# One core, chunked attention, routed attention and a feed-forward layer: the attention tick as a list of single-engine operations, one order for each kind of tick

## Chip, core and metric

One core of a Trainium2 chip runs the whole program. The time is the device time of one execution in microseconds (us); lower is better. PE is the matmul engine, PEld its weight loads, DVE the vector engine, ACT the activation engine, POOL the general-purpose engine (GpSimd), SP the engine whose queue issues the DMAs.

## What is computed

The reference, cut to what matters (B = 8, H = 8, S = 576, D = 64, so 4608 rows of width 512):

```python
# 1. attention inside chunks of 64 rows, for each head
scores = scale * np.matmul(q_c, k_c.transpose(0, 1, 2, 4, 3))
attn = softmax(scores)                    # max subtracted, sum + 1e-9
x = np.matmul(attn, v_c)                  # rows of 512 = 8 heads x 64
# 2. four experts of causal attention over all 576 rows, top 2 of 4 per row
for e in range(4):
    q, k, v = x @ wq[e], x @ wk[e], x @ wv[e]
    a = softmax(where(causal, -1e9, scale * q @ k.T))
    out += gate_weight[e] * (a @ v @ wo[e])
# 3. layer norm, 512 -> 2048 -> 512 with relu, residual
return x + np.maximum(xn @ w_ch1, 0.0) @ w_ch2
```

`w_ch1` and `w_ch2` arrive as float64 and are narrowed to float32 on the core with integer operations.

## The kernel before

The 4608 rows are 36 tiles of 128 rows, nine to a pair of sequences. After a prologue the first two parts run together in **ticks**. Tick `s` (from 7 on) works on several tiles at once, each at another stage:

- chunk attention of tile `s`: scores on PE (`chunk_scores`), maximum and shift on DVE and exponential on ACT (`chunk_soft`), row sums on DVE and the scaling of `pc` on POOL (L168, `chunk_norm`), transposes on PE (`pT_ps`, L174) copied by ACT to `pTc` (L176, `chunk_turn`); then, one tick later, the values (`chunk_values`, L186, which reads `pTc`) and their split into a high part (ACT, L195) and a low part (DVE, L196);
- a share of the projections of three tiles (`proj_group`): matmuls into `pp` (L237) or `pv` (L258), then the high part on ACT and the low part on DVE (`kWl` L251, `ql` L241, for `pv` the copy `lg` L261);
- expert attention of tile `g = s - 7`: scores `sp` on PE (L345) for two pairs of experts, mask and negated maximum on DVE (L358), exponentials on ACT (L364), sums and gate weights `l` on DVE (L373 to L375), and the weighting of `P` on POOL (L379, `attn_weigh`);
- tile `g - 1`: transposes of `P` into `tp` on PE (L390), copied out half by ACT (L392) and half by DVE (`pTa`, L394);
- tile `g - 2`: values `oa_ps` on PE (L409), their high part `zh` on ACT and low part `zl` on DVE (L412), then the output projection `y_ps` (L419), copied by ACT (L422) and sent off by SP.

The number of key blocks differs: a tile has one to five of 128 keys, by its place in its pair of sequences. Ticks in which the scores are over 512 columns wide (the fifth and the ninth tile of each pair of sequences) are **wide**: their second pair of experts is scored late in the tick, after the transposes, since each wide score tile takes a buffer of its own. Every third tick has a third projection step.

PSUM, the matmuls' output memory, is shared in two pools: `pss` has three buffers (`sp`, `sx_ps` of the chunk attention, `tp`), `ps` has two (`pT_ps`, `pp`, `pv`, `oa_ps`, `y_ps`). A matmul into a buffer waits until the readers of its last contents are done.

In ticks 7 to 36 the order on PE, DVE, ACT and POOL is the order in which `tick` is written (`manual_schedule`); an instruction that waits holds up all that stand behind it on its engine. SP's DMAs are placed by a scheduler. Ticks 37 to 44, in which the layer norm of the third part is begun (`fill`), and the third part itself are ordered by the scheduler on all engines.

The narrowing of `w_ch1`, 16 blocks of 128x512, runs in the ticks' background (`narrow`, called through `bg`, seven steps a tick): a load, four DVE steps (L438, L440, L442, L444), an addition on POOL (L446), two DVE steps (L451, which waits for the addition, and L456), two multiplications on ACT (L460), four combinations on POOL (L469), a store. One block is begun when the one before it is finished, 16 steps later; what is left at the end of tick 36 is put out there at once (`bg(s, 999)`). The narrowing of `w_ch2` runs in the third part and uses the same helper.

The heart of the order before is:

```python
        if last:
            zhigh, zlow = attn_values(g - 2)
            zhigh()
        ...
        if live:
            attn_weigh(g, 0, 1 if late2 else EP)
        if zlow:
            zlow()
        if s < NT:
            chunk_norm(s)
```

Of the kernel before, what the change touches and what calls it, by code (L numbers as in the profile page):

```python
# [7 lines left out]
F32 = mybir.dt.float32  # L8
# [14 lines left out]
def tile_kernel(ctx, tc, dims, qkt, vt, wqt, wkt, wvt, wo, g_ln, w_ch1, w_ch2, out):  # L23
# [118 lines left out]
    probs, turned, valued = {}, {}, set()  # L142
# [10 lines left out]
    def chunk_soft(g, acc):  # L153
        nm = se.tile([128, 2, HP], F32, name="nmc", bufs=3)
        nc.vector.tensor_reduce(nm, acc, AX.X, OP.max, negate=True)
        pc = se.tile([128, HP, 2, C], F32, name="pc", bufs=2)
        nc.vector.tensor_tensor(pc.rearrange("p h b j -> p b h j"), acc, nm[:, :, :, None].to_broadcast([128, 2, HP, C]), OP.add)
        pw = pc.rearrange("p h b j -> p (h b j)")
        nc.scalar.activation(pw, pw, AF.Exp, scale=scale)
        probs[g] = pc  # L160

    def chunk_norm(g):
        pe = probs[g].rearrange("p h b j -> p (h b) j")
        l = se.tile([128, H], F32, name="lc", bufs=3)
        nc.vector.tensor_reduce(l, pe, AX.X, OP.add)
        nc.vector.tensor_scalar(l, l, 1e-9, None, OP.add)
        nc.vector.reciprocal(l, l)
        nc.gpsimd.tensor_tensor(pe, pe, l[:, :, None].to_broadcast([128, H, C]), OP.mult)  # L168

    def chunk_turn(g):  # L170
# [4 lines left out]
        pT = se.tile([128, HP, 128], F32, name="pTc", bufs=2)  # L175
        nc.scalar.activation(pT, pT_ps, AF.Copy)  # L176
        turned[g] = pT

    def chunk_values(g, acc):
        pT, vb = turned.pop(g), loaded.pop(g)[1]  # L180
        valued.add(g)
# [6 lines left out]
    def chunk_high(g, acc):  # L188
# [6 lines left out]
        nc.scalar.activation(xh, src, AF.Copy)  # L195
        return lambda: nc.vector.tensor_tensor(xl, src, f32(xh), OP.subtract)  # L196
# [4 lines left out]
    def early_scores(g):  # L201
        acc = pair_tile(pss, "s_ps", "ps2")[:, :, :HP, :]
        chunk_scores(g, acc)
        chunk_soft(g, acc)
        chunk_norm(g)

    def early_values(g):
        acc = pair_tile(pss, "x_ps", "ps2")[:, :, :HP, :]
        chunk_values(g, acc)
        valued.remove(g)  # L210
        chunk_high(g, acc)()
# [3 lines left out]
    HALF = (slice(0, HD), slice(HD, 2 * HD))  # L215

    def proj_group(gi):
# [13 lines left out]
        def rows_(ep, isq):  # L231
            wh, wl = (wqh, wql) if isq else (wkh, wkl)
            ws = slice(ep * 128, (ep + 1) * 128)
            pp = ps.tile([128, GW], F32, name="pp", tag="ps")
# [4 lines left out]
            if isq:  # L239
                nc.scalar.activation(qh[:, ep, :], pp, AF.Copy)  # L240
                nc.vector.tensor_tensor(ql[:, ep, :], pp, f32(qh[:, ep, :]), OP.subtract)  # L241
                return
            for w, base, end in ((0, 0, WK), (1, S, 2 * S)):
                lo_, hi_ = max(t0, base), min(t0 + GW, end)
                if lo_ >= hi_:
                    continue
                kh, kl = kWs[p, w]
                src = pp[:, lo_ - t0:hi_ - t0]
                ds = slice(lo_ - base, hi_ - base)
                nc.scalar.activation(kh[:, ep, ds], src, AF.Copy)  # L250
                nc.vector.tensor_tensor(kl[:, ep, ds], src, f32(kh[:, ep, ds]), OP.subtract)  # L251

        def vals(j):
            pv = ps.tile([128, VW], F32, name="pv", tag="ps")
# [5 lines left out]
            nc.scalar.activation(vg[:, j, :], pv[:, :NV], AF.Copy)  # L260
            nc.vector.tensor_copy(lg[:, j, :], pv[:, NV:])  # L261

        for fn, arg in ((rows_, (0, False)), (rows_, (0, True)), (rows_, (1, False)), (vals, (0,)), (rows_, (1, True)), (vals, (1,)),
                        (vals, (2,))):
            fn(*arg)
            if (fn, arg) != (vals, (GT - 1,)):
                yield
# [47 lines left out]
    def attn_scores(g, ep):  # L315
# [23 lines left out]
        for si in range(len(views[0][1])):  # L339
            for x, y, first, last in ((ql, kh, True, False), (qh, kl, False, False), (qh, kh, False, True)):  # L340
                for e2 in range(2):
# [24 lines left out]
        return exps  # L366

    def attn_weigh(g, e0, e1):
        p, t, w, n = split_of(g)
# [5 lines left out]
        nc.vector.tensor_tensor(l, l, wg, OP.mult)  # L375
        for ep in range(e0, e1):
# [684 lines left out]
```

## Time and profile before

| | us |
|---|---|
| median of 3 runs (lowest, highest) | 1254.93 (1252.5, 1255.03) |
| the profiled execution, own time | 1253.89 |
| its span, first to last instruction | 1251.9 |
| PE busy | 1201.5 (96%) |
| DVE busy | 899.3 (72%) |
| ACT busy | 580.0 (46%) |
| POOL busy | 258.4 (21%) |

The prologue ends about 51 us after the span's start; ticks 7 to 36 take from there to about 424 us, ticks 37 to 44 to about 500 us, and the third part the rest. A busy share is an average over these parts. Matmuls are pipelined and their ends are modelled, so PE's idle time and the waits that ended it say more than its busy time. The granted clock is the share of full speed at which the throttle let PE run.

### The profile page before, as it was taken

What the parts mean: (1) busy time and instruction counts of PE and PEld (TensorE: products, weight loads), DVE (VectorE), ACT (ScalarE), POOL (GpSimd) and SP (SyncE); (2) the same over time, 40 slices, a digit from 0 to 9 for tenths busy, and PEclk for the clock granted to TensorE, in tenths of its full rate; (3) what the DMA queues carried; (4) which work ended last, traced back from release to release, by engine and by line L of the source; (5) the groups of instructions that cost most, each with busy time, mean ns of one, the idle gap of its engine ahead of it and who ended that gap; (6) DMA issues with size and microseconds to landing.
All of it is one profiled execution on the core that took longest, in us unless ns stands there. A gap on an engine that the chain in (4) does not pass through costs nothing.

```text
span 1251.9 us, 29166 instructions
## 1 busy us (share of the span) xinstructions
PE 1201.5 (96%) x11874; PEld 1140.7 (91%) x11874; DVE 899.3 (72%) x1837; ACT 580.0 (46%) x1115; POOL 258.4 (21%) x480
## 2 busy tenths in 40 slices
PE   7999999999999889999999999999799999999998
PEld 5888887988888777999999999999799999999998
DVE  5687877787787678777657765755797778767782
ACT  3465665565556548633334433445443333324341
POOL 2244444443443534121112111210000000000000
PEclk9999999999999999999999999999999999999999
DMA  8233333333331225655554645557864445554521
GB/s 275 89 121 108 124 126 123 115 125 118 124 108 51 90 99 191 219 183 187 171 181 158 189 163 178 167 169 250 318 193 161 152 151 162 169 175 140 165 95 41
DMA packets 95845, 191.69 MB, mean 153 GB/s; under 512 B 8544, under 2 KB 42336, under 8 KB 94816
## 3 DMA queue, kind: packets, MB, share of 16 engines
q1 hardware_dynamic: 95712, 189.83, 45.8%
q8 instruction: 93, 1.52, 0.5%
q14 instruction: 40, 0.33, 0.1%
HBM read 118.50 MB, written 71.30 MB: 152 GB/s over the span
## 4 chain that ended last, share of the span: by engine, by line
PE 50%; DMA 3%; DVE 1%; issue 0%; SPq 0%; ACT 0%; DVEq 0%; ACTq 0%
PE bb L958 16%; PE bb L768 12%; PE ad L958 12%; PE ad L768 9%; PE tp L659 1%; DMA hx<-hd 1%; DMA w2u<-w2d 1%; DMA xc<-xs 0%; DMA raw<-in_w_ch 0%; SPq L776 0%; DVE hxc L918 0%; DVE hx L917 0%; DVE xr L968 0%; SPq L931 0%; DVE u L792 0%
## 5 line engine op out<-in xcount | busy, mean ns | idle before, releaser
L768 PE MATMUL bb<-x,w1u 128*128 128x256 f32 x1728 | 217.5, 281 | 3.4 <-ACT v L789 2.2
L768 PEld LDWEIGHTS bb<-x,w1u 128*128 128x128 f32 x1728 | 209.7, 188 | 4.6 <-ACT v L789 2.6
L768 PE MATMUL ad<-x,w1u 128*128 128x256 f32 x1296 | 173.7, 283 | 0.6 <-DVE v L792 0.6
L768 PEld LDWEIGHTS ad<-x,w1u 128*128 128x128 f32 x1296 | 160.6, 188 | 1.2 <-DVE v L792 0.8
L958 PE MATMUL bb<-w2u,hn 128*128 128x256 f32 x928 | 159.9, 280 | 0.8 <-DVE xr L968 0.8
L958 PEld LDWEIGHTS bb<-w2u,hn 128*128 128x128 f32 x928 | 134.0, 189 | 1.0 <-DVE xr L968 1.0
L958 PE MATMUL bb<-w2u,hx 128*128 128x256 f32 x640 | 125.5, 283 | 0.5 <-DVE hx L923 0.5
L379 POOL TENSOR_SCALAR P<-P,l 128x128 f32<-128x128 f32 (+8 forms) x144 | 87.3, 624 | 148.4 <-DVE l L375 118.0
L364 ACT ACTIVATE P<-P,nm 128x128 f32<-128x128 f32 (+8 forms) x144 | 87.1, 607 | 48.5 <-DVE nm L358 45.1
L958 PE MATMUL ad<-w2u,hn 128*128 128x256 f32 x632 | 104.4, 281 | 0.0
L958 PEld LDWEIGHTS bb<-w2u,hx 128*128 128x128 f32 x640 | 100.9, 191 | 0.7 <-DVE hx L923 0.7
L446 POOL TENSOR_TENSOR cvt<-cva,cvt 128x512 f32<-128x512 f32 x32 | 46.7, 1459 | 257.8 <-DVE cvt L444 220.0
L958 PEld LDWEIGHTS ad<-w2u,hn 128*128 128x128 f32 x632 | 89.3, 189 | 0.0
L958 PE MATMUL ad<-w2u,hx 128*128 128x256 f32 x504 | 88.9, 280 | 0.0
L469 POOL TENSOR_TENSOR cw<-cw 128x128 f32<-128x128 f32 x128 | 60.7, 494 | 66.3 <-issue 50.8
L958 PEld LDWEIGHTS ad<-w2u,hx 128*128 128x128 f32 x504 | 74.1, 189 | 0.0
L358 DVE CUSTOM_DVE_ANT_0 P<-sp,mcaus 128x128 f32<-128x128 f32 (+7 forms) x128 | 60.2, 519 | 3.5 <-PE sp L345 3.3
L409 PE MATMUL oa_ps<-pTa,vg 128*64 128x128 f32 x928 | 59.7, 279 | 0.0
L390 PE MATMUL tp<-ident,P 128*128 128x128 f32 x464 | 57.7, 273 | 1.9 <-POOL P L379 1.9
L677 DVE TENSOR_TENSOR x<-xt,x 128x512 fp32r<-128x512 f32 x63 | 45.3, 729 | 18.9 <-ACT x L676 18.9
L390 PEld LDWEIGHTS tp<-ident,P 128*128 128x128 f32 x464 | 52.5, 141 | 4.9 <-POOL P L379 3.4
L409 PEld LDWEIGHTS oa_ps<-pTa,vg 128*64 128x64 f32 x928 | 50.7, 138 | 3.9 <-issue 1.4
(244 smaller groups left out, 2609.9 us busy)
## 6 DMA issues: line engine op xcount, KB each, us to landing
qk<-in_qk SPq DMA_DIRECT2D x36, 512.0 KB, 4.2
hn<-hd SPq DMA_DIRECT2D x34, 512.0 KB, 4.2
raw<-in_w_ch SPq DMA_DIRECT2D x32, 512.0 KB, 3.7
hx<-hd SPq DMA_DIRECT2D x29, 512.0 KB, 4.6
vb<-in_v SPq DMA_DIRECT2D x36, 256.0 KB, 4.3
xs<-y SPq DMA_DIRECT2D x36, 256.0 KB, 2.2
xc<-xs SPq DMA_DIRECT2D x18, 512.0 KB, 4.5
hd<-p SPq DMA_DIRECT2D x36, 256.0 KB, 4.2
```

Of the source, the lines that this page charges most:

```text
L358: nc.vector.tensor_tensor_reduce(dst, src, mk, -1.0, -3.0 * NEG, OP.add, OP.min, nm[:, e2:e2 + 1])
L364: nc.scalar.activation(pe, pe, AF.Exp, bias=nm[:, e2:e2 + 1], scale=-1.0, accum_out=l[:, e2:e2 + 1])
L379: nc.gpsimd.tensor_scalar(pe, pe, l[:, ep - e0, e2:e2 + 1], 1.0, OP.mult, OP.mult)
L390: nc.tensor.transpose(tp[:, i, :], P[ep][e2][:, kt * 128:(kt + 1) * 128], ident)
L409: nc.tensor.matmul(o_ps[e2 * HD:(e2 + 1) * HD, ep, :], vg[:, gk % GT, e * HD:(e + 1) * HD], pT[:, e * n + kt, :], start=(kt == 0), stop=(k ...
L446: nc.gpsimd.tensor_tensor(t.bitcast(F32), a.bitcast(F32), t.bitcast(F32), OP.add)
L469: nc.gpsimd.tensor_tensor(w[:, o, :], w[:, x, :], w[:, y, :], op)
L659: nc.tensor.transpose(tp[:, f, :], xc[:, i, f * 128:(f + 1) * 128], ident)
L677: nc.vector.tensor_tensor(t[:, 1], tsum[i], f32(t[:, 0]), OP.subtract)
L768: nc.tensor.matmul(out[:, p], w[:, kt, a, WI[i], :], x[:, b_, kt, :], start=(start and p == 0 and kt == 0 and q == 0), stop=False, skip_gr ...
L958: ins = nc.tensor.matmul(to[:, t], x[:, c, ts], w2u[i][:, w, half * 4 + c, :], start=start, stop=False, skip_group_check=True)
```

## The change

`tick` is cut into operations that each work on one engine, under short names, and the order of a tick is a string of these names. There are four strings: for ordinary ticks (`""`), for ticks with a third projection step (`"3"`), for wide ticks (`"w"`) and for wide ticks with a third step (`"3w"`). The names:

- on PE: `S0`, `S1` scores of the two pairs of experts, `C` chunk scores and values, `O` values of `g - 2`, `P` and `Q` projection, `T` transposes (with their copies), `Y` output projection, `K` chunk transposes;
- on DVE: `D0`, `D1` mask and maximum, `N` chunk maximum and shift, `X` low part of the chunk values, `z` is `zl`, `R` chunk sums, `v` low part of a projection, `L`, `L1` the sums `l`;
- on ACT: `E0`, `E1` exponentials, `H` high part of the chunk values, `Z` is `zh`, `n` chunk exponential, `a` high part of a projection, `y`, `k` the copies of `y_ps` and `pT_ps`;
- on POOL: `r` scaling of `pc`, `W`, `W1` the weighting of `P`;
- `G1` to `G3` steps of the gate, `F0`, `F1` the layer norm's steps, `B` one beat of the narrowing.

`Q` takes its PSUM buffer from the pool of three. A projection onto keys that crosses two sequences now makes both high parts first and then both low parts.

The narrowing is a table of beats instead of a chain of steps: a block begins every 13 beats and its last step stands 18 beats after its load, so that two blocks overlap at their ends. POOL's addition is at beat 5 and the DVE step that reads it at beat 9 (before: 2 steps later, now 4), the last DVE step at 10 and ACT's multiplications at 13 (before: 1 step later, now 3). `cva` has two buffers for `w_ch1`. Seven beats a tick as before; one is run before tick 7, and at most 16 after tick 36.

```diff
+    BEAT = {-2: "load", 1: "v1", 2: "v2", 3: "v3", 4: "v4", 5: "add", 9: "v6", 10: "v7", 13: "gain", 14: "s0", 15: "s1", 16: "store"}
+    PERIOD = 13
...
+    beat = [-2]
+
     def bg(s, n=1):
         for _ in range(n):
-            if s < CS:
-                return
-            if not cgen:
-                if not conv:
-                    return
-                cgen.append(conv.pop(0)())
-            if next(cgen[0], 0) == 0:
-                cgen.pop()
+            beat[0] += 1
+            for k, parts in enumerate(conv):
+                name = BEAT.get(beat[0] - 1 - PERIOD * k)
+                if name:
+                    parts[name]()
+
+    PLAN = {
+        "": "S0 S1 C D0 E0 D1 H G2 N O B Z X E1 n z R r P a v B T B G3 F0 L B Y P y a W B F1 B v K k B",
+        "3": "S0 D0 S1 E0 C H G2 D1 N E1 O X Z P G3 z n R r B a v Q a v L W B F0 T Y B y P a v B G1 B B K k F1 B",
+        "w": "S0 D0 C E0 O P Z N z n H X R r F0 S1 a D1 v E1 L B L1 Y y T B P B W B B a v W1 K B F1 B k",
+        "3w": "S0 C D0 H N E0 O Z X n P R z Q a v r a v S1 L D1 T B Y B F0 W B y E1 B P a v L1 G1 K B W1 k B B F1",
+    }
...
-        if late2:
-            attn_scores(g, 1)()
-            attn_weigh(g, 1, EP)
-        if last:
-            attn_out(g - 2)
...
+        for op in PLAN[("3" if three else "") + ("w" if wd else "")].split():
+            if op in do:
+                do[op]()
         if s == MID - 1:
-            bg(s, 999)
-        if fill is not None:
-            fill(s, 1)
+            bg(s, 16)
```

Three places in the two built programs. First PE in tick 20, a wide one, from the projection of the keys on (`tp` are the transposes of `P`, `sp` the scores). Before:

```order
L237 MATMUL pp<-xTh,wkh 128x384
L390 MATMUL tp<-ident,P 128x128 x16
L345 MATMUL sp<-kWh,ql 128x320 x2
L345 MATMUL sp<-kWl,qh 128x320 x2
L345 MATMUL sp<-kWh,qh 128x320 x2
```

And now:

```order
L358 MATMUL sp<-kWh,qh 128x320 x2
L438 MATMUL y_ps<-woh,zl 128x512
L438 MATMUL y_ps<-wol,zh 128x512
L438 MATMUL y_ps<-woh,zh 128x512
...
L409 MATMUL tp<-ident,P 128x128 x16
L273 MATMUL pv<-wvh,xTl 128x260
```

The late scores, and behind them the output projection, now stand ahead of the transposes.

Second DVE in tick 19, an ordinary one, from the chunk maximum to the copy of the transposes. Before:

```order
L155 TENSOR_REDUCE nmc<-sx_ps 128x8
L157 TENSOR_TENSOR pc<-sx_ps,nmc 128x2x4x64
L295 TENSOR_REDUCE den<-ex 128x3
L296 TENSOR_SCALAR den<-den 128x3
L297 RECIPROCAL den<-den 128x3
L196 TENSOR_TENSOR xTl<-sx_ps,xTh 128x4x128
L373 TENSOR_SCALAR l<-l 128x4
L374 RECIPROCAL l<-l 128x4
L375 TENSOR_TENSOR l<-l,wg 128x4
L412 TENSOR_TENSOR zl<-oa_ps,zh 128x256
L165 TENSOR_REDUCE lc<-pc 128x8
```

And now:

```order
L155 TENSOR_REDUCE nmc<-sx_ps 128x8
L157 TENSOR_TENSOR pc<-sx_ps,nmc 128x2x4x64
L196 TENSOR_TENSOR xTl<-sx_ps,xTh 128x4x128
L431 TENSOR_TENSOR zl<-oa_ps,zh 128x256
L165 TENSOR_REDUCE lc<-pc 128x8
L166 TENSOR_SCALAR lc<-lc 128x8
L167 RECIPROCAL lc<-lc 128x8
L264 TENSOR_TENSOR kWl<-pp,kWh 128x384
L413 COPY pTa<-tp 128x512
L308 TENSOR_REDUCE den<-ex 128x3
```

The gate's three operations on `den` and the three on `l` no longer stand ahead of `zl`; they follow the copy of the transposes.

Third POOL around tick 19. Before:

```order
L299 TENSOR_TENSOR wg<-ex,den 128x12
L379 TENSOR_SCALAR P<-P,l 128x512 x4
L168 TENSOR_TENSOR pc<-pc,lc 128x512
L446 TENSOR_TENSOR cvt<-cva,cvt 128x512
L379 TENSOR_SCALAR P<-P,l 128x640 x2
```

And now (ticks 17 and 18, where the same pair of operations stands):

```order
L171 TENSOR_TENSOR pc<-pc,lc 128x512
L479 TENSOR_TENSOR cvt<-cva,cvt 128x512
L398 TENSOR_SCALAR P<-P,l 128x256 x4
L171 TENSOR_TENSOR pc<-pc,lc 128x512
L398 TENSOR_SCALAR P<-P,l 128x384 x4
```

The scaling of `pc` now comes ahead of the weighting of `P` of the same tick.

## Rows read from the trace of the kernel before

**Rows 1.** Windows: busy us of each engine, granted clock, DMA share, GB/s.

```profile
83.00:195.00 112.00, 108.05 (x1389) 96.50 (x1386) 86.04 (x247) 66.80 (x167) 47.98 (x96) 0.98 0.35 119
195.00:308.00 113.00, 107.82 (x1396) 96.22 (x1395) 85.78 (x250) 66.97 (x168) 47.88 (x96) 1.00 0.34 116
308.00:412.00 104.00, 99.74 (x1273) 89.13 (x1271) 78.12 (x227) 60.25 (x151) 42.83 (x88) 0.98 0.28 95
412.00:500.00 88.00, 77.87 (x639) 65.68 (x638) 65.83 (x191) 55.12 (x131) 36.99 (x74) 0.94 0.37 130
```

**Rows 2.** Waits of PE from 51 to 500: total us, times, longest.

```profile
PE sp L345 <- DVE pTa L394: 7.6, 7, 2.4
PE sx_ps L186 <- ACT pTc L176: 5.3, 5, 1.8
PE y_ps L419 <- DVE zl L412: 4.0, 4, 2.1
PE pT_ps L174 <- POOL pc L168: 4.0, 2, 2.1
PE pv L258 <- DVE lg L261: 2.0, 1, 2.0
PE tp L390 <- POOL P L379: 1.9, 3, 0.9
```

**Rows 3.** Windows just behind two waits of PE, columns as in rows 1.

```profile
155.00:160.00 5.00, 4.22 (x19) 3.42 (x20) 3.83 (x12) 2.50 (x6) 0.00 (x0) 0.66 0.33 105
...
211.00:216.00 5.00, 3.86 (x66) 3.62 (x67) 2.90 (x7) 3.90 (x10) 0.00 (x0) 1.00 0.68 251
```

**Rows 4.** Timeline of PE in tick 20: start, us, instruction, idle before and releaser.

```profile
212.14 0.69 PE L186 MATMUL sx_ps<-pTc,vb 64*64 64x64 f32 x32 [1.82 <-ACT pTc L176]
...
219.19 0.41 PE L345 MATMUL sp<-kWh,ql 64*128 64x320 f32 x1 [0.50 <-DVE pTa L394]
```

**Rows 5.** Timeline of POOL in tick 19.

```profile
206.87 1.04 POOL L168 TENSOR_TENSOR pc<-pc,lc 128x512 f32<-128x512 f32 x1
207.87 1.27 POOL L446 TENSOR_TENSOR cvt<-cva,cvt 128x512 f32<-128x512 f32 x1
```

**Rows 6.** Timeline of DVE in tick 19.

```profile
201.81 0.16 DVE L295 TENSOR_REDUCE den<-ex 128x3 f32<-128x12 f32 x1
...
202.30 0.66 DVE L196 TENSOR_TENSOR xTl<-sx_ps,xTh 128x512 fp32r<-128x512 f32 x1
202.88 0.16 DVE L373 TENSOR_SCALAR l<-l 128x4 f32<-128x4 f32 x1
...
203.44 0.42 DVE L412 TENSOR_TENSOR zl<-oa_ps,zh 128x256 fp32r<-128x256 f32 x1
...
209.17 0.43 DVE L451 TENSOR_SCALAR cva<-raw 128x512 int32<-128x512 int32 x1 [2.23 <-POOL cvt L446]
```

**Rows 7.** Timeline of ACT at the end of tick 19.

```profile
210.70 0.91 ACT L460 ACTIVATE cw<-cva,gk 128x256 f32<-128x256 f32 x2 [2.00 <-DVE cva L456]
211.51 0.57 ACT L176 ACTIVATE pTc<-pT_ps 128x512 f32<-128x512 f32 x1
```

**Rows 8.** Timeline of POOL in tick 7.

```profile
56.79 1.41 POOL L379 TENSOR_SCALAR P<-P,l 128x128 f32<-128x128 f32 x4 [0.88 <-DVE l L375]
58.16 1.04 POOL L168 TENSOR_TENSOR pc<-pc,lc 128x512 f32<-128x512 f32 x1
```

**Rows 9.** Timeline of DVE behind tick 36.

```profile
425.92 0.68 DVE L440 SCALAR_TENSOR_TENSOR cva<-raw,cva 128x512 int32<-128x512 int32 x1
...
435.17 1.06 DVE L440 SCALAR_TENSOR_TENSOR cva<-raw,cva 128x512 int32<-128x512 int32 x1
```

**Rows 10.** Timeline of POOL behind tick 36.

```profile
434.83 3.89 POOL L379 TENSOR_SCALAR P<-P,l 128x512 f32<-128x512 f32 x4
```

**Rows 11.** Groups of DVE from 51 to 457: busy us, mean ns, idle before.

```profile
L440 DVE SCALAR_TENSOR_TENSOR cva<-raw,cva 128x512 int32<-128x512 int32 x16 | 12.7, 795 | 0.3
```

**Rows 12.** Waits of DVE from 51 to 500.

```profile
DVE lg L261 <- ACT vg L260: 26.3, 20, 2.9
```

More of the change, by code (lines that the diff above doesn't have):

```diff
@@ L140, in tile_kernel @@
     groups = {}
-    probs, turned, valued = {}, {}, set()
+    probs, lcs, turned = {}, {}, {}
     ROWS = (slice(0, C), slice(C, 2 * C))
@@ L209, in early_values @@
         chunk_values(g, acc)
-        valued.remove(g)
-        chunk_high(g, acc)()
+        for f in chunk_split(g, acc):
+            f()
     qTs, kWs, vgs, wgs = {}, {}, {}, {}
@@ L447, in narrow @@
[L447 to L462 removed]
+        t_ = {}
@@ L501, in tick @@
             projs.append(proj_group((s - GT - 1) // GT))
-        live, last = 0 <= g < NT, 0 <= g - 2 < NT
-        late2 = live and wide(g)
-        xlow = zhigh = zlow = exps = None
-        if live:
-            attn_scores(g, 0)()
-            if not late2:
-                exps = attn_scores(g, 1)
-        step(gates[0] if gates else None)
-        old = s - 1 in turned
-        if old or s < NT:
+        live, wd = 0 <= g < NT, 0 <= g < NT and wide(g)
+        three = (s - GT - 1) % GT == 2
@@ new lines, in tick, with scores, proj, turn_off @@
+        do, highs, lows = {}, [], []
+        def scores(ep):
+            do[f"D{ep}"], do[f"E{ep}"] = attn_scores(g, ep)
+        def proj(big=False):
+            if projs:
+                if big:
+                    wide_bank.append(1)
+                high, low = next(projs[0])
+                highs.append(high)
+                lows.append(low)
+                if big:
+                    wide_bank.pop()
+        def turn_off():
+            if projs and three:
+                next(projs.pop(0), None)
+            step(gates[0] if gates else None)
@@ new lines, in tick @@
+        if s < NT or s - 1 in turned:
+            do["C"] = chunk
+        if 0 <= g - 2 < NT:
+            do["O"], do["Y"] = values, out_
+        if 0 <= g - 1 < NT:
+            do["T"] = lambda: attn_turn(g - 1)
+        if s < NT:
+            do["K"] = turn
+        do["P"], do["Q"], do["G1"] = proj, (lambda: proj(True)), turn_off
+        do["a"] = lambda: highs and highs.pop(0)()
+        do["v"] = lambda: lows and lows.pop(0)()
+        do["G2"], do["G3"] = (lambda: step(gates[0] if gates else None)), (lambda: step(gates.pop(0) if gates else None))
```

266 lines of the change are left out of this document (137 added, 129 removed).

## Prediction

> **What bounds the kernel now.** I read the windows by stage first. From 83 to 412 us, 26 whole ticks, PE is busy for 315.6 of 329 us, and 77.9 of 88 behind that [rows 1]. No other engine comes near: DVE, the next, has 249.9 of the 329. So the matmuls set the pace, their number is not changed, and what an order can give back is PE's idle time and the clock that it loses. The third part, over half of the span, keeps its order on PE and gives nothing.
>
> Then the waits of PE [rows 2]. The six largest between 51 and 500 us sum to 24.8 us. Each is a wait for one step of another engine, not for a busy one: late scores for a copy of the transposes, chunk values for `pTc`, the output projection for `zl`, chunk transposes for the scaling of `pc`.
>
> Third, the clock. Behind the wait that ended at 155.8 the granted clock is 0.66 over five us; behind that at 212.1 it stays 1.00 [rows 3]. 0.66 of five us is a stretch of 3.4 us at 1.2 GHz, which loses (1 - 0.66) x 5 = 1.7 us of full speed. Seven such stretches lie between 51 and 500 us, each behind one of the waits of rows 2: 7 x 1.7 = 11.9. So all that can be won is 24.8 + 11.9 = 36.7 us, 2.9%.
>
> **The change, part by part.**
>
> Wide ticks. The late scores wait because the transposes just ahead of them have taken the buffers of the pool of three, and DVE copies these out late: 7 waits, 7.6 us, one of them in rows 4. Now the late scores and the output projection stand ahead of the transposes (in `"3w"` only the scores). Their two buffers were those of the first scores, which DVE reads within 2 us, behind 5 us of other matmuls. What is late next is the transposes' second buffer, which DVE's first pass over the late scores frees: that pass is done about when eight transposes are through, so I leave 0.15 us a tick, 1.0 in all. Gain 6.6.
>
> Chunk values and the narrowing. In tick 19 POOL does the scaling of `pc` and then the narrowing's addition, which ends at 209.14 [rows 5]. DVE's next narrowing step has waited 2.23 us for it [rows 6], the multiplications on ACT wait 2.00 us for the step after that, and the copy `pTc` stands behind them until 211.51 [rows 7]; PE waits 1.82 us for it [rows 4]. This is the pattern of the 5.3 us in five waits. With four beats instead of two between addition and reader, and three instead of one ahead of ACT, each step has half a tick; ACT no longer stands still ahead of `pTc`. One place is left: in `"3w"` ACT does `E1` behind `y`, and `pTc` comes out about when the next tick wants it. I leave 0.6. Gain 4.7.
>
> `zl`. DVE did the gate's `den` (0.49 us, from the first start to the next row's) and `l` (0.56) ahead of `zl` [rows 6], and `l` can wait for exponentials besides. Both now stand behind it, which is 1.05 us earlier, but one more narrowing step (0.68, the shorter of rows 9) may stand ahead in its place. The wait of 0.64 in tick 19 becomes about 0.64 - 1.05 + 0.68 = 0.3. Four waits, 4.0 us in all, leave 1.2. Gain 2.8.
>
> First ticks. The scaling of `pc` started at 58.16, right behind 1.41 us of weighting, which now follows it [rows 8]. DVE reaches the chunk sums earlier too, by the same 1.05. POOL can then begin when the sums are there, some 1.4 us sooner than before, and of 2.1 us there stay about 0.6; in tick 8, where the weighting is longer, about 0.4. Of 4.0 us there go 3.0. The price is a later weighting, which the next tick's transposes read; they come over 5 us into that tick, so it is covered unless POOL is over 3 us behind.
>
> Behind tick 36. Three of 16 narrowings ran there in one go, with DVE steps wedged between those of the attention [rows 9]. They now run inside the ticks. The longest waits of two rows above are there and are counted there; one more, `pv` for `lg`, 2.0 us, loses its cause in part, since the second projection takes its buffer from the other pool: gain 1.0. The 1.9 us of `tp` for POOL stay.
>
> The waits sum to 6.6 + 4.7 + 2.8 + 3.0 + 1.0 = 18.1. Of the seven slow stretches five should go (the three in wide ticks, the one at `zl` behind tick 36, one of the first two): 5 x 1.7 = 8.5.
>
> Against it: three more narrowings in the ticks. Six DVE steps of at most 0.795 us, the costliest kind [rows 11], are 4.8 us a block, 14 us in all. DVE has 329 - 249.9 = 79 us free in the 26 ticks, 3.0 a tick, so most of it is covered; in the shortest ticks, of 10 us, it is not. With such ticks, and waits of the new strings that no row of before shows, I charge 4 us; the bounds are 0 and, if every tick pays half a microsecond, 13. Moving PE's groups costs nothing: the number of changes between kinds of matmuls in a tick stays. The load of the first block moves ahead of tick 7, at the same place in SP's queue.
>
> DVE and POOL get in each other's way: the same narrowing step took 0.68 us alone and 1.06 us [rows 9] while POOL weighted `P` for 3.89 us [rows 10]. The Trainium skill, page "SBUF — State Buffer", section "Who interferes with whom", says that a DVE instruction with two SBUF inputs or in a two-port mode and a GpSimd one that reads SBUF exclude each other, whichever starts second waiting. The trace agrees with a hold of 0.38 us. Were every one of a block's six steps held so, it would be 2.3 us a block; the mean of rows 11 is only 0.12 above 0.68, so spread steps are held in a third of cases, and I stay with my 4.
>
> The sum: 1253.9 (the profiled execution) - 18.1 - 8.5 + 4 = 1231.3. The median of the runs is 1.0 above the profiled one: **1232 us**.
>
> **Rivals.**
>
> 1. Only the narrowing's part comes true. The strings remove waits at one place and make them at another (the transposes' second buffer, `pv` for a late `v`, `zl` behind a narrowing beat). Then go the 4.7 of `pTc`, the 2.4 and 2.1 that are the longest of two rows [rows 2] and the 1.0, with three slow stretches behind tick 36 (5.1), less the 4: 11.3, or 1244. For it: waits of PE are a few tenths, and orders of other engines shift by as much as a narrowing step. Against it: the seven buffer waits have a cause that is gone from PE's queue.
>
> 2. The gain is given back: both effects cancel within 2.5 us, 1254. This needs new waits of over half a microsecond in every tick, which a slack of some microseconds at most of the moved steps speaks against.
>
> 3. Slower: DVE's queue becomes the bound. DVE waits at the head of its queue too, 26.3 us in 20 waits for `vg` alone, 1.3 each [rows 12]; a strict new order, with more beats inside, can add such waits. If each of the 26 ticks had one more of 1.3 that reached PE, that is 34 us against 26.6 won: 1261. It decides when waits and narrowing together use up DVE's 3.0 free us a tick. Against it: `l`, which waited for ACT, and the step that waited for POOL are moved to where their input is long there.
>
> **How the numbers follow.** The forecast, 1226 to 1238, has 0.58; rival 1, to 1249, 0.24; rival 2, 0.09; rival 3, 0.09. The lower end, 1220, is near 1253.9 - 36.7 + 1.0 = 1218, when every wait goes; the upper end, 1249, takes in rival 1 and the charge of 13. Outside stand rivals 2 and 3. A measurement of this kernel can tell 0.2%, 2.5 us, from no change: faster 0.82, same 0.09, slower 0.09.
>
> **What would show it.** Right: no wait of `sp` for a copy of the transposes; chunk values without a wait over 0.5 us for `pTc`; the waits of `zl` and `pc` down to tenths; no narrowing step of `w_ch1` behind tick 36; at most two stretches at 0.66 between 51 and 500 us; the chunk attention's last tick some 12 us earlier. Wrong: new groups among PE's waits with a sum over 10 us, above all `tp` for DVE or POOL and `pv` or `pp` for a low part; DVE busy over nine tenths of a tick with PE waiting; or slow stretches that stay although the waits are gone.

## The result and the profile after

The changed kernel takes 1215.15 us in the median (1213.76 to 1216.4) beside 1254.43 for the kernel before: a ratio of 0.9689, with an interval of 0.9672 to 0.9706. The profiled execution took 1214.83 us, its span 1213.1. The forecast was 1232 us, and the time lies under the range (1220 to 1249): the sign was right, and the gain of 39 us is more than the 36.7 that the prediction called all that can be won.

PE's waits in ticks 7 to 44 of the changed kernel (us in total, times, longest) answer to [rows 2]:

```profile
PE pT_ps L177 <- DVE l L389: 3.4, 1, 3.4
PE y_ps L438 <- DVE zl L431: 2.2, 3, 1.2
PE tp L409 <- POOL P L398: 1.3, 2, 0.9
PE sp L358 <- DVE pTa L413: 1.1, 1, 1.1
PE pT_ps L177 <- POOL pc L171: 0.9, 1, 0.9
```

`sp` waits for a copy of the transposes once (7.6 us in seven waits before), the chunk values no longer wait for `pTc` (5.3 in five), `zl` is at 2.2 (4.0 in four). The chunk transposes still wait 4.3 us (4.0): this term brought nothing.

Windows of the changed kernel (columns as in [rows 1]) behind its one long wait, and at the place of [rows 3]:

```profile
65.00:70.00 5.00, 3.64 (x29) 2.87 (x32) 4.15 (x14) 1.33 (x4) 3.42 (x5) 0.54 0.31 107
70.00:75.00 5.00, 5.00 (x85) 4.71 (x80) 3.44 (x9) 4.02 (x13) 0.00 (x0) 0.78 0.47 159
155.00:160.00 5.00, 5.00 (x55) 4.79 (x52) 4.67 (x16) 3.85 (x14) 2.08 (x5) 1.00 0.75 258
```

One slow stretch is left in the ticks, of twice the length ((1 - 0.54) x 5 + (1 - 0.78) x 5 = 3.4 us lost), where there were seven of 1.7.

Now the two halves of the attention as windows: from the chunk scores of tick 7 to those of tick 35, and from there to the first matmul of the third part. Before:

```profile
51.60:402.10 350.50, 333.49 (x4258) 298.04 (x4256) 267.61 (x782) 206.02 (x517) 147.75 (x298) 0.98 0.33 113
402.10:501.00 98.90, 88.43 (x795) 75.14 (x793) 74.31 (x215) 61.51 (x148) 40.71 (x79) 0.95 0.34 121
sum 449.40, PE 421.92 PEld 373.18 DVE 341.92 ACT 267.53 POOL 188.46; mean PE 210.96 PEld 186.59 DVE 170.96 ACT 133.76 POOL 94.23
```

After:

```profile
49.70:378.50 328.80, 323.52 (x4254) 293.69 (x4252) 278.11 (x799) 205.77 (x521) 166.06 (x309) 0.99 0.37 128
378.50:465.60 87.10, 82.53 (x812) 71.07 (x810) 67.05 (x200) 64.43 (x147) 33.48 (x68) 1.00 0.32 114
sum 415.90, PE 406.05 PEld 364.76 DVE 345.16 ACT 270.21 POOL 199.54; mean PE 203.02 PEld 182.38 DVE 172.58 ACT 135.10 POOL 99.77
```

The stretch is 449.4 - 415.9 = 33.5 us shorter. PE's idle time in it falls from 449.40 - 421.92 = 27.5 to 415.90 - 406.05 = 9.9, that is by 17.6. PE's *busy* time falls too, by 15.9 us, for the same matmuls. Of that the clock explains 7 x 1.7 - 3.4 = 8.5; 7.4 are left, for the most part waits that no row of idle time shows (the section "Waits that the idle time doesn't show"). The other 5.3 us of the 38.8 by which the spans differ lie in the prologue (1.9) and the third part (3.4).

### The profile page after: what moved, and what is told of

The parts are those of the page before. It is cut to its first block, busy times and chain, and to the rows that moved or that the text cites. A ratio compares the mean times of both kernels' runs of the same rounds, so it can differ in the third digit from the quotient of the medians.

```text
span 1213.1 us, 29176 instructions
## 1 busy us (share of the span) xinstructions
PE 1182.9 (98%) x11874; PEld 1130.0 (93%) x11874; DVE 903.9 (75%) x1837; ACT 581.7 (48%) x1117; POOL 267.8 (22%) x480
## 4 chain that ended last, share of the span: by engine, by line
PE 86%; DVE 7%; DMA 3%; ACT 1%; issue 1%; POOL 1%; SPq 0%; ACTq 0%; DVEq 0%; POOLq 0%
PE bb L1023 16%; PE bb L833 16%; PE ad L1023 12%; PE ad L833 12%; PE pp L246 7%; PE pv L273 4%; PE y_ps L438 4%; PE oa_ps L428 4%; PE tp L409 3%; PE sp L358 3%; PE tp L724 2%; PE sx_ps L151 1%; DMA w2u<-w2d 1%; PE pT_ps L177 1%; DVE P L376 1%; PE sx_ps L187 1%
## 5 line engine op out<-in xcount | busy, mean ns | idle before, releaser
L381 ACT ACTIVATE P<-P,nm 128x128 f32<-128x128 f32 (+8 forms) x144 | 87.2, 608 | 44.3 <-DVE nm L376 37.0
L398 POOL TENSOR_SCALAR P<-P,l 128x128 f32<-128x128 f32 (+8 forms) x144 | 94.8, 676 | 39.7 <-DVE l L391 24.9
L509 POOL TENSOR_TENSOR cw<-cw 128x128 f32<-128x128 f32 x128 | 64.8, 526 | 57.7 <-issue 48.4
L171 POOL TENSOR_TENSOR pc<-pc,lc 128x512 f32<-128x512 f32 x36 | 37.8, 1052 | 140.0 <-DVE lc L167 83.1
```

The source lines that it names most:

```text
L381: nc.scalar.activation(pe, pe, AF.Exp, bias=nm[:, e2:e2 + 1], scale=-1.0, accum_out=l[:, e2:e2 + 1])
L398: nc.gpsimd.tensor_scalar(pe, pe, sums_[g][:, ep, e2:e2 + 1], 1.0, OP.mult, OP.mult)
L509: nc.gpsimd.tensor_tensor(w[:, o, :], w[:, x, :], w[:, y, :], op)
```

## Experiments

Chips differ a little (the kernel before had medians of 1254.4 to 1257.2 us in the six comparisons), so kernels are compared by their ratio to the kernel before on the same chip, and "us" in the table are ratio x 1254.4. Ticks 7 to 34 and 35 to 44 are the two windows above, from the profiled executions; idle time and waits are those of PE over 0.15 us in the first. The clock is not taken out: in ticks 7 to 34 it costs 6.8 us before, 3.4 in the changed kernel, and 0 (skip7, block0_late) to 8.5 (only_narrowing, only_wide) elsewhere.

| kernel | ratio (interval) | against before | ticks 7 to 34: us, idle, waits | 35 to 44 |
|---|---|---|---|---|
| before | 1 | 0 | 350.5, 16.7, 21 | 98.9 |
| only_narrowing | 0.9988 (0.9971 to 1.0005) | -1.5 | 359.8, 22.5, 24 | 88.4 |
| only_wide | 1.0015 (1.0003 to 1.0027) | +1.9 | 354.5, 21.9, 18 | 101.9 |
| only_wide_y | 0.9970 (0.9955 to 0.9985) | -3.8 | 348.7, 17.2, 25 | 102.6 |
| high_only | 0.9948 (0.9931 to 0.9966) | -6.5 | 345.4, 12.8, 21 | 101.7 |
| wide_high | 0.9915 (0.9890 to 0.9940) | -10.7 | 342.8, 15.3, 18 | 100.7 |
| three_edits | 0.9902 (0.9878 to 0.9926) | -12.3 | 352.0, 19.2, 23 | 88.5 |
| wide_back | 0.9799 (0.9783 to 0.9815) | -25.2 | 337.7, 11.0, 9 | 89.8 |
| old_narrowing | 0.9795 (0.9781 to 0.9810) | -25.7 | 332.6, 7.4, 7 | 95.4 |
| skip7 | 0.9753 (0.9731 to 0.9776) | -31.0 | 332.4, 9.3, 11 | 91.6 |
| dist_back | 0.9739 (0.9718 to 0.9759) | -32.7 | 334.1, 9.9, 8 | 87.5 |
| l_back | 0.9734 (0.9706 to 0.9763) | -33.4 | 333.4, 8.0, 7 | 87.0 |
| skip78 | 0.9719 (0.9689 to 0.9749) | -35.2 | 332.0, 7.3, 10 | 87.1 |
| block0_late | 0.9691 (0.9668 to 0.9714) | -38.8 | 327.4, 5.2, 6 | 87.3 |
| high_back | 0.9689 (0.9667 to 0.9712) | -39.0 | 331.1, 7.0, 7 | 87.2 |
| changed kernel | 0.9689 (0.9672 to 0.9706) | -39.0 | 328.9, 5.1, 3 | 87.1 |
| after_again | 0.9689 (0.9674 to 0.9705) | -39.0 | 327.4, 5.0, 3 | 87.3 |
| y_back | 0.9678 (0.9648 to 0.9709) | -40.4 | 328.2, 5.3, 4 | 86.8 |
| block0_mid_y | 0.9682 (0.9662 to 0.9702) | -39.9 | 327.0, 4.8, 5 | 87.2 |
| block0_mid | 0.9671 (0.9656 to 0.9686) | -41.3 | 325.9, 4.5, 4 | 87.2 |

### Each half alone, and each half undone

only_narrowing puts the new table of beats into the kernel before; old_narrowing puts the old chain into the changed kernel:

```diff
-    BEAT = {-2: "load", 1: "v1", 2: "v2", 3: "v3", 4: "v4", 5: "add", 9: "v6", 10: "v7", 13: "gain", 14: "s0", 15: "s1", 16: "store"}
-    PERIOD = 13
+    BEAT = {-1: "load", 0: "v1", 1: "v2", 2: "v3", 3: "v4", 4: "add", 7: "v6", 8: "v7", 9: "gain", 10: "s0", 11: "s1", 13: "store"}
+    PERIOD = 16
...
-            bg(s, 16)
+            bg(s, 999)
```

> The kernel before with the narrowing's table of beats alone (old order of every tick). Theory A (a wait of PE costs its idle row plus some 0.3 us that no row of idle time shows): it takes away the waits for pTc (5.3 us by the rows), the two longest for zl and pTa behind tick 36 (2.1 and 2.4) and half of lg (1.0), 10.8 us in 8 waits, with 8 x 0.3 = 2.4 unseen, and three slow stretches (5.1): 1254.4 - 18.3 = 1236. Theory B (the rows are complete, and what the change gained beyond them came from the narrowing, which no longer stands in DVE's and POOL's way): 10.8 + 5.1 + the 13 us that the forecast missed: 1226.

> The changed kernel with the old chain of narrowing steps (16 steps a block, the old distances, one buffer, the rest put out behind tick 36); the new strings stay. Theory A: the strings alone give what the narrowing doesn't, 39.3 - 18.3 = 21.0: 1233. Theory B: they give the row sum of the wide ticks, zl and pc, 6.6 + 0.8 + 3.0 and two slow stretches, some 14: 1240. The rival of the prediction in which only the narrowing's part comes true: 1251 or more.

only_wide moves the late scores alone in the kernel before, wide_back moves them (and in `"w"` the output projection) back in the changed one:

```diff
+        if late2:
+            attn_scores(g, 1)()
         if 0 <= g - 1 < NT:
             attn_turn(g - 1)
...
         if late2:
-            attn_scores(g, 1)()
             attn_weigh(g, 1, EP)
```

```diff
-        "w": "S0 D0 C E0 O P Z N z n H X R r F0 S1 a D1 v E1 L B L1 Y y T B P B W B B a v W1 K B F1 B k",
-        "3w": "S0 C D0 H N E0 O Z X n P R z Q a v r a v S1 L D1 T B Y B F0 W B y E1 B P a v L1 G1 K B W1 k B B F1",
+        "w": "S0 D0 C E0 O P Z N z n H X R r F0 a v L B T B S1 D1 E1 L1 Y y P B W B B a v W1 K B F1 B k",
+        "3w": "S0 C D0 H N E0 O Z X n P R z Q a v r a v L T B S1 D1 Y B F0 W B y E1 B P a v L1 G1 K B W1 k B B F1",
```

> The kernel before with one edit: in wide ticks the scores of the second pair of experts, with their mask, maximum and exponential, stand ahead of the transposes. Theory A: 7 waits of sp, 7.6 us by the rows, and 7 x 0.3 = 2.1 unseen, less 1.0 left, and two or three slow stretches (3.4 to 5.1): 1254.4 - 13 = 1241; the span without its clock loss falls by 8.7, PE's idle time by only 6.6. Theory B: the span without its clock loss falls by as much as PE's idle time, 6.6, and the time is 1243 to 1244.

> The changed kernel with the late scores and the output projection of wide ticks behind the transposes again (in the ticks with a third step only the scores); all else as changed. Theory A: waits of sp for pTa come back, some 7 of about 1 us, with 0.3 unseen each, and two or three slow stretches: 1215.2 + 13 = 1228, and the span without its clock loss grows by some 2 us more than PE's idle time. Theory B: 7.6 + 3.4: 1226, with both growing alike.

Undone, each half costs 13 to 14 us; alone, they give 1.5 and -1.9. Theory A's figures for the halves undone hold within 3 us (1233 and 1228 expected, 1230.1 and 1231.0 measured), those for the halves alone do not: the gains do not add up, and neither theory had that.

For the narrowing the table shows where it goes: in ticks 35 to 44 it gives 10.5 us in the old order and 8.3 in the new, but in ticks 7 to 34 it costs 9.3 in the old order (1.7 of it clock) and nothing in the new (332.6 us with the old chain, 328.9 with the table of beats). For the wide ticks, the first wait of PE in only_wide:

```profile
PE tp L390 <- DVE nm L358: 9.8, 5, 3.1
```

One of them:

```profile
271.88 1.09 PE L390 MATMUL tp<-ident,P 128*128 128x128 f32 x8 [2.14 <-DVE nm L358]
```

The wait of `sp` is gone and the transposes wait instead, for the buffer of the very scores that were moved, which DVE has not yet masked. This is what the prediction priced at 0.15 us a tick.

### What makes DVE late in a wide tick

DVE in that tick of only_wide (24, with a third step), up to the mask for which PE waits, and ACT ahead of it:

```profile
266.27 0.69 DVE L155 TENSOR_REDUCE nmc<-sx_ps 128x8 f32<-128x512 f32 x1 [1.56 <-ACT xTh L195]
...
271.07 0.75 DVE L358 CUSTOM_DVE_ANT_0 P<-sp,mcaus 128x576 f32<-128x576 f32 x1
```

```profile
264.91 0.76 ACT L364 ACTIVATE P<-P,nm 128x576 f32<-128x576 f32 x1
265.57 0.18 ACT L364 ACTIVATION_READ_ACCUMULATOR P<-P,nm 128x1 f32 x1
265.67 0.57 ACT L195 ACTIVATE xTh<-sx_ps 128x512 fp32r<-128x512 f32 x1
```

The same tick of the changed kernel, which starts at 246.96 instead of 262.81:

```profile
248.82 0.69 DVE L155 TENSOR_REDUCE nmc<-sx_ps 128x8 f32<-128x512 f32 x1 [0.31 <-ACT xTh L196]
```

```profile
248.19 0.60 ACT L196 ACTIVATE xTh<-sx_ps 128x512 fp32r<-128x512 f32 x1 [0.72 <-PE sx_ps L187]
248.68 0.77 ACT L381 ACTIVATE P<-P,nm 128x576 f32<-128x576 f32 x1
```

The chunk maximum waits for `xTh`, which reads the other half of the same buffer, and `xTh` stood behind the exponentials of the first pair. In the changed kernel these follow it (`"3w"`) or the maximum comes ahead of it (`"w"`): the maximum starts 1.9 us into the tick instead of 3.5. The prediction named the place on PE and did not look at ACT. Five kernels separate the two. y_back and only_wide_y vary the output projection; high_only, wide_high and high_back vary the order on ACT:

```diff
-            attn_scores(g, 0)()
+            exps = attn_scores(g, 0)
             if not late2:
+                exps()
                 exps = attn_scores(g, 1)
```

That is high_only, an edit of the kernel before; wide_high has it and the edit of only_wide. Next y_back and high_back, on the changed kernel (in high_back also `H N` behind `E0` in `"3w"`):

```diff
-        "w": "S0 D0 C E0 O P Z N z n H X R r F0 S1 a D1 v E1 L B L1 Y y T B P B W B B a v W1 K B F1 B k",
+        "w": "S0 D0 C E0 O P Z N z n H X R r F0 S1 a D1 v E1 L B L1 T B Y y P B W B B a v W1 K B F1 B k",
...
+        "w": "S0 D0 C E0 H N O P Z z n X R r F0 S1 a D1 v E1 L B L1 Y y T B P B W B B a v W1 K B F1 B k",
```

only_wide_y is only_wide with `attn_out(g - 2)` of wide ticks right behind the late scores.

> The changed kernel with one edit, in wide ticks without a third step: the late scores stay ahead of the transposes, but the output projection goes behind them again, as it was. Theory C (it is the output projection between late scores and transposes that hides DVE's pass over the late scores, whose buffer the transposes take): tp waits for the masked scores in four ticks, some 2 us each, with 0.35 a wait unseen and one or two slow stretches: 1215.2 + 12 = 1227. Theory D (the late scores alone do it, and the waits of the kernel with only that edit came from DVE's old order): 1215 to 1218.

> The kernel before with the late scores and the output projection of all wide ticks ahead of the transposes, all else as before. Theory C: of the 9.8 us in which tp waited for the masked scores some 7 go, with some unseen time and two slow stretches: 1257.3 - 12 = 1245. Theory D: DVE's old order (the gate and the sums ahead of zl) makes the output projection wait for zl instead: no gain, 1253 or more.

> The changed kernel with one edit in wide ticks: ACT does the exponentials of the first pair (E0) ahead of the high part of the chunk values (H), and DVE's chunk maximum (N) follows behind H, as before; the places of scores, transposes and output projection stay as changed. Theory E (in wide ticks it was this order on ACT that made DVE late by some 1.5 us, since the chunk maximum waits until H has read the shared buffer, and every wait of a wide tick hangs on DVE): the masked late scores come 1.5 us later and tp or y_ps wait for DVE in the eight wide ticks, about 1 us each with 0.35 unseen and two slow stretches: 1215 + 13 = 1228. The rival (it was the place of the late scores on PE, as the prediction had it): 1215 to 1218.

> The kernel before with one edit: in wide ticks the exponentials of the first pair stand behind the high part of the chunk values on ACT instead of ahead of it. Theory E: DVE does the chunk maximum 1.5 us earlier in wide ticks, and the 7.6 us in which sp waits for pTa and the waits for zl there fall by more than half: 1254.7 - 8 = 1246. The rival: nothing, 1253 or more.

> The kernel before with both edits in wide ticks: the late scores ahead of the transposes, and the first pair's exponentials behind the high part of the chunk values. Theory E: of the 9.8 us in which tp waited for the masked scores 7 go, with the 7.6 of sp gone as there: 1257.3 - 13 = 1244. The rival: the two do no more than each alone, 1250 or more.

Theory C falls for the changed kernel: there the output projection may stand on either side (y_back). In the old order it counts in part. only_wide_y is 5.7 us faster than only_wide, half of the 12 that C expected: the transposes wait for the masked scores 1.3 us in one wait instead of 9.8 in five, as C had it, but the output projection now waits for `zl` 7.9 us in nine waits instead of 4.5 in five, as D had it. High_only takes more than half of the `sp` waits away, without a matmul moved:

```profile
PE sp L345 <- DVE pTa L394: 3.6, 5, 2.4
```

So theory E holds for the kernel before: the swap on ACT gives 6.5 us, and with it the late scores, which alone cost 1.9, give 4.2 more. In the changed kernel the order on ACT does not matter (high_back; the 1228 of theory E did not come), while the place of the scores does (wide_back). That DVE has time enough there for the old order on ACT is likely, but not shown.

What else gives DVE time? l_back puts the gate's last step and the sums back ahead of `zl` in ticks that are not wide, and three_edits adds the narrowing's table to wide_high:

```diff
-        "": "S0 S1 C D0 E0 D1 H G2 N O B Z X E1 n z R r P a v B T B G3 F0 L B Y P y a W B F1 B v K k B",
+        "": "S0 S1 C D0 E0 D1 H G2 N O B Z X E1 G3 L n z R r P a v B T B F0 B Y P y a W B F1 B v K k B",
```

(l_back has the same in `"3"`.)

> The changed kernel with the gate's last step and the sums l ahead of zl and of the chunk sums again in ticks that are not wide; all else as changed. By the prediction's terms: 2.8 for zl and up to 3.0 for pc in the first ticks come back: 1219 to 1221, with PE's waits for zl and pc longer by 4 to 6 us. The rival (with all 16 blocks inside the ticks DVE is later than before the change, and the sums wait for the exponentials at the queue's head): over 1225. A third: nothing, under 1217, if DVE is ahead of PE by the microsecond anyway.

> The kernel before with three edits and none of the new strings: late scores ahead of the transposes, first pair's exponentials behind the high part of the chunk values in wide ticks, and the narrowing's new table of beats. If DVE's slack in wide ticks is what the narrowing lacked, it now gives behind tick 36 its 10 us and loses half of the 9 us that it lost inside the ticks: 1247 - 6 = 1241. If few edits give most of the gain: 1230 or less. If the rest of the list is needed for the narrowing to be free: 1246 or more.

l_back costs 5.6 us, with `y_ps` waiting 5.8 us for `zl` in six waits instead of 2.2 in three. Three_edits came out near the 1241 that the first case expected, but not for its reason: the narrowing gives 12.3 us in ticks 35 to 44 and loses 9.3 in ticks 7 to 34, all of what it lost without the edits (342.8 to 352.0). So these two edits of the wide ticks are not what makes the narrowing free. DVE's own waits at its queue's head (us, times, longest, ticks 7 to 44) fit the view that the order of DVE as a whole makes it free, but do not show it. Before, besides [rows 12]:

```profile
DVE nmc L155 <- ACT xTh L195: 21.0, 26, 2.1
DVE ql L241 <- ACT qh L240: 11.8, 10, 2.4
DVE l L373 <- ACT P L364: 11.1, 11, 1.3
DVE cva L451 <- POOL cvt L446: 10.9, 8, 2.3
```

After:

```profile
DVE lg L276 <- ACT vg L275: 23.2, 19, 2.3
DVE nmc L155 <- ACT xTh L196: 10.9, 21, 1.5
DVE ql L264 <- ACT qh L260: 4.5, 5, 1.6
...
DVE l L389 <- ACT P L381: 1.8, 3, 1.2
```

These four go from 54.8 to 17.2 us (the last has no row left). In only_narrowing they are still 42.4 (19.8, 7.9, 10.0, 4.7). DVE's busy time in ticks 7 to 34 grew by 10.5 (278.11 - 267.61 in the windows above). These sums do not tell cause from effect. DVE's idle time in ticks 7 to 44 is their length less its busy time, 449.4 - 341.9 = 107.5 us before and 415.9 - 345.2 = 70.7 after: whatever makes the ticks 33.5 us shorter, with 3.3 us more work, takes 36.8 from it. Shown is that the two edits of the wide ticks are not enough (three_edits) and that the place of the gate's last step and the sums is worth 5.6 us (l_back). Which other entries of the list let the narrowing run for nothing was not tried one by one, and stays open.

### The beats

dist_back has the old distances inside a block, a block still every 13 beats. (From POOL's addition to the DVE step that reads it they are three steps, not the two that the description of the change and the prediction give: `add` and `v6` stand at 4 and 7 in the old chain above.)

```diff
+    BEAT = {-2: "load", 1: "v1", 2: "v2", 3: "v3", 4: "v4", 5: "add", 8: "v6", 9: "v7", 10: "gain", 11: "s0", 12: "s1", 14: "store"}
```

> The changed kernel with the old distances inside a block (the DVE step that reads POOL's addition 3 beats behind it instead of 4, ACT's multiplications 1 beat behind DVE's last step instead of 3), a block still every 13 beats and nothing more behind tick 36 than before. By the prediction's second term: the waits of chunk values for pTc come back inside the ticks, some 3 us in three or four waits, with 0.37 each unseen and one slow stretch: 1215 + 6 = 1221. The rival (packing the blocks is all the gain): 1215 to 1217.

It costs 6.3 us as expected, but by other waits: `pTc` has 0.6 us in one wait; the chunk transposes' buffer waits 2.8 us for the copy of `y_ps` on ACT, and `zl` has 3.6 instead of 2.2. The distance counts, and what a late step meets on its queue was guessed wrong.

The 3.4 us wait in tick 8 was not foreseen. In tick 7 DVE did four narrowing steps ahead of the masks of tick 8 (the last row here), and all behind them came late:

```profile
55.40 1.01 DVE L465 TENSOR_SCALAR cva<-raw 128x512 int32<-128x512 int32 x1
...
57.37 0.69 DVE L468 SCALAR_TENSOR_TENSOR cva<-raw,cva 128x512 int32<-128x512 int32 x1
58.09 0.49 DVE L471 TENSOR_SCALAR cvt<-cva 128x512 int32<-128x512 int32 x1
58.61 0.73 DVE L475 SCALAR_TENSOR_TENSOR cvt<-raw,cvt 128x512 f32<-128x512 uint32 x1
...
59.74 0.41 DVE L376 CUSTOM_DVE_ANT_0 P<-sp,mcaus 128x256 f32<-128x256 f32 x1
```

```profile
66.36 1.11 PE L177 MATMUL pT_ps<-ident,pc 128*128 128x128 f32 x4 [3.36 <-DVE l L389]
```

Three kernels take those steps away: skip7 (no beat in tick 7, all blocks seven beats later), skip78 (none in ticks 7 and 8, a block every 12 beats, and a beat moved behind `zl`), block0_late (the first block alone seven beats later, with second buffers for the raw block and `cvt`; its line of beats is shown):

```diff
-                name = BEAT.get(beat[0] - 1 - PERIOD * k)
+                name = BEAT.get(beat[0] - 1 - (PERIOD * k or 7))
```

> The changed kernel with no beat of the narrowing in tick 7, so that seven more are put out behind tick 36; beats 13 apart and all strings as changed. In the kernel without beats in ticks 7 and 8, tick 8 fell from 11.96 to 8.26 us and PE's wait in it from 3.36 to 1.08, but it lost 6 us in later ticks, where beats every 12 stood at other places. Expected: tick 8 shorter by 3 us, tick 9 by 1.1 without the slow stretch, behind tick 36 up to 1 us more: 1215.2 - 3 = 1212. The rival (any shift of the beats against the ticks makes waits, three steps of a tick in 39 being as near as they were): 1218 or more.

> The changed kernel with no beat of the narrowing in ticks 7 and 8 (a block every 12 beats instead of 13 makes up for it), and in ordinary ticks the first beat behind zl instead of ahead of it. The wait of 3.36 us in tick 8 is late by the four narrowing steps (2.9 us) that stand ahead of DVE's masks there: it falls by some 2 us, and the slow stretch behind it (up to 3.4 us long lost at half speed, 1.7) may go; the wait of 0.77 for zl in tick 19 goes. Expected 1215.2 - 2.0 - 0.8 - 0.4 = 1212, 1210 if the slow stretch goes. The rival: the first ticks are bound by the chunk attention's chain of steps from scores to transposes, and the wait stays: 1214.

> The changed kernel with the first of the 16 blocks 7 beats, one tick, later than its place in the table, and two buffers for the raw block and for cvt so that it may overlap the second; every other beat stands where it stood. Ticks 7 to 9 as in the kernel without beats in tick 7: 27.4 instead of 32.2 us, since DVE no longer does four narrowing steps ahead of the masks of tick 8; tick 9 or 10 loses up to 1.0 by the steps that now stand there; from tick 11 on as the changed kernel. Expected 1215.2 - 4 = 1211. The rival (later ticks make new waits as with the other shifts): 1218.

All three shorten tick 8 from 12.0 to 8.3 us. skip7 and skip78 lose more than that in ticks 12 to 34 (7.3 and 8.1 us). skip7 loses 4.5 more in ticks 35 to 44, 3.4 of it clock; seven more beats are put out behind tick 36 there. PE's waits in skip7 begin with these:

```profile
PE y_ps L438 <- DVE zl L431: 4.7, 5, 1.7
PE sx_ps L187 <- ACT pTc L179: 2.8, 2, 2.3
```

That beats now stand at bad places in the later ticks is read from such waits and was not tried by itself. block0_late gives 3.4 us back at once, in ticks 10 and 11: six DVE steps of two blocks now stand in tick 9, ahead of the masks of tick 10. From tick 12 to 34 it takes 273.4 us, as the changed kernel does. block0_mid spreads the steps, beside the changed kernel itself on the same chip (block0_mid_y has y_back's edit as well):

```diff
+    BEAT0 = {-2: "load", 5: "v1", 6: "v2", 7: "v3", 8: "v4", 9: "add", 12: "v6", 13: "v7", 16: "gain", 17: "s0", 18: "s1", 19: "store"}
...
+                name = (BEAT if k else BEAT0).get(beat[0] - 1 - PERIOD * k)
```

> The changed kernel with the steps of the first block of the narrowing alone spread otherwise: its four DVE steps from the last beat of tick 7 through tick 8, the addition behind them, the last two DVE steps at the end of tick 8 and the start of tick 9; two buffers for raw block and cvt; all other beats as changed. If the steps ahead of the masks were the cause: ticks 7 to 9 fall from 32.2 to about 27.5 us, ticks 10 and 11 stay within 0.5 of 23.2, and the time is 4 us under the changed kernel on this chip: 0.9660 of before. The rival (each place in these ticks costs as much as it gives): within 0.2% of the changed kernel, as block0_late.

> The same with the output projection of wide ticks without a third step behind the transposes. The kernel with that edit alone came out 1.4 us under the changed kernel, less than a measurement can tell: as block0_mid within 2 us.

> The changed kernel itself on this chip: a ratio to before of 0.9672 to 0.9706, as first measured; its prologue and its third part, where the profiled run stood 1.9 and 3.4 us under before, within the spread of the other kernels (prologue 49.7 to 53.1, third part 746.0 to 751.4), so that these 5 us belong to the run and not to the change.

block0_mid takes 1213.41 us (1213.25 to 1214.42), the changed kernel there 1215.67 (1215.53 to 1217.02): the fastest kernel, 2.3 us under it at the medians, although the intervals of the ratios overlap. Ticks 7 to 9 fall to 28.3 us from 32.2 (31.2 in after_again), but tick 10 still grows by 1.0 (1.4), with a wait of 1.19 for `zl`; 0.5 at most and a time 4 us lower had been expected. So the steps ahead of the masks were the cause in tick 8, and a quarter to a half of what they cost there comes back. block0_mid_y took 1214.27, within 2 us as expected.

### Waits that the idle time doesn't show

Tick 20 in wide_back and in the changed kernel, PE from the late scores to the output projection:

```profile
211.28 0.41 PE L358 MATMUL sp<-kWh,ql 64*128 64x320 f32 x1
212.88 0.41 PE L358 MATMUL sp<-kWh,ql 64*128 64x320 f32 x1 [1.20 <-DVE pTa L413]
...
213.95 0.50 PE L438 MATMUL y_ps<-woh,zl 128*128 128x512 f32 x1
```

```profile
204.58 0.41 PE L358 MATMUL sp<-kWh,ql 64*128 64x320 f32 x2
204.83 0.31 PE L358 MATMUL sp<-kWl,qh 64*128 64x320 f32 x2
...
205.66 0.50 PE L438 MATMUL y_ps<-woh,zl 128*128 128x512 f32 x1
```

From the first of these matmuls to the output projection it is 2.67 us with the wait and 1.08 without: the wait cost 1.59, its row says 1.20. Undisturbed, the row of the first two matmuls is shown 0.41 us long and the next row starts 0.25 after it: shown lengths overlap, and the part of a wait that falls under the last matmul shown counts as busy. Over all 20 profiled kernels of this study, the length of ticks 7 to 34 less PE's idle time and the clock's loss is 319.6 + 0.35 x (number of waits over 0.15 us), with a correlation of 0.97. By this line 18 waits fewer are worth 6.2 us that no row lists.

The kernels with many waits are those with the old order, so the line alone does not say that the waits are the cause. The traces do, step by step. Take the distance between the starts of two matmuls with a wait between them, less the wait's row, less the same distance undisturbed at full clock: it is 0.07 to 0.41 us, 0.20 in the mean of 227 waits. In ticks 7 to 34 this sums to 5.1 us for the 21 waits of the kernel before and to 0.6 for the three of the changed one. Delays too short for a row give another 1.5 us, and the undisturbed distances of the two orders of PE differ by 0.6 in sum. So the 0.35 holds more than what lies under a wait's own row, and tick 20 is near the top of the range.

## Why the prediction was wrong, by its own steps

- **Where to look** was right: the third part and the prologue are not changed. The 1.9 us of the prologue are no gain: in another run of the same kernel (after_again) it took 52.8 us, beside 49.7 here and 51.6 before. Third parts of all kernels lie between 746.0 and 751.4, in the mean 749.4 with the old order of the ticks and 747.7 with the new strings, so 1 or 2 us there may belong to the change. With the ticks (33.5 us, 34.6 in after_again) that is less than the 39 us of the medians: some 3 to 4 us are not placed.
- **The sum of the waits** came out, 18.1 forecast and 17.6 measured, but in part by luck: the terms miss by up to 3.3 us and cancel. Wide ticks: 6.6 forecast, 6.5 by the rows. `pTc`: 4.7, and 5.3 came. `zl`: 2.8, and 1.8. First ticks: 3.0, and -0.3; the narrowing's steps ahead of the masks of tick 8 were left out of this term. `pv`: 1.0, and 2.0. These make 15.3; 0.6 came at `tp` for POOL, which was to stay, and 1.7 at waits outside the six rows.
- **The clock** was right in sum: 5 x 1.7 = 8.5, and 8.5 came. By stretches it was not: six went and the one that is left is twice as long (in after_again it is 1.7).
- **The ceiling failed.** 24.8 + 11.9 was called all that can be won, since idle time was taken for the whole price of a wait. Beyond idle time and clock PE's busy time fell by 7.4 us more, most of it the parts of waits that no row shows.
- **The charge of 4 us failed.** It was reckoned from DVE's free time of 3.0 us a tick as if that were slack, to be paid for the most part in the shortest ticks. In the old order the three blocks cost 9.3 us in ticks 7 to 34 (only_narrowing), in the new one nothing could be seen of them. What in the new list does this stays open beyond the 5.6 us of l_back.
- 17.6 - 18.1 = -0.5 for the waits, 4.0 for the charge, 7.4 for what no row shows and 5.3 outside the ticks make the 16.2 us by which the profiled span lies under the sum. The first three are steps of the prediction, 10.9 us together; the 5.3 are none.
- **The cause in wide ticks** was half right: buffers and place on PE as named, but alone they move the wait to the transposes; the order on ACT was missed.
- **Rivals.** The first (only the narrowing's part comes true) is turned round: without the narrowing the strings give 25.7 us, and the narrowing alone 1.5. The second and third did not come; nearest to the third's mechanism, more work in DVE's strict order that reaches PE, is only_narrowing. What the prediction took from the Trainium skill (page "SBUF — State Buffer", section "Who interferes with whom") did not grow into a cost with the blocks inside the ticks. Of the three steps with two inputs that of [rows 11] takes 774 ns in the changed kernel (795 before) and the other two 806 and 794 (745 and 720); all six steps of a block together take 3.98 us, 4.08 before.

The changed kernel's rows for these three, in the ticks, and those of the other two before:

```profile
L475 DVE SCALAR_TENSOR_TENSOR cvt<-raw,cvt 128x512 f32<-128x512 uint32 x16 | 12.9, 806 | 0.3
L489 DVE SCALAR_TENSOR_TENSOR cva<-cva,cvt 128x512 f32<-128x512 f32 x16 | 12.7, 794 | 0.2
L468 DVE SCALAR_TENSOR_TENSOR cva<-raw,cva 128x512 int32<-128x512 int32 x16 | 12.4, 774 | 0.2
```

```profile
L444 DVE SCALAR_TENSOR_TENSOR cvt<-raw,cvt 128x512 f32<-128x512 uint32 x16 | 11.9, 745 | 0.2
L456 DVE SCALAR_TENSOR_TENSOR cva<-cva,cvt 128x512 f32<-128x512 f32 x16 | 11.5, 720 | 0.2
```

## What to carry to other kernels

Price a wait of PE by the distance between matmul starts in a disturbed and an undisturbed stretch, not by its idle time. Before work is added to an engine, do not take its free time for slack: ask which late step will stand behind the new work in its queue (three blocks cost 9.3 us in one order of DVE and nothing in another), and follow an order on every engine that feeds the late step. Parts of a reordering are worth different amounts alone and together: undoing each part of the finished version says what it is worth there (13 to 14 us each here), and adding it alone to the old one may say nothing of that (1.5 and -1.9).

## What had not been expected of the hardware

The granted clock differs between executions of one program: the changed kernel lost 3.4 us of full speed in the prologue in one profile and 5.1 in another, and two stretches more or less there and in the third part move the time by as much as some of the edits. And a wait of PE has a part, 0.20 us in the mean of 227 waits and 0.41 at most, that lies under the matmul shown ahead of it.
